# Riding projections on gate/up tails, a GpSimd memset that orders row halves, and a first norm ahead of the weight copies

## The chip, the cores and the metric

One core of one Trainium2 chip runs the kernel. The metric is the device time in microseconds of one execution, lower is better. The engines are PE (TensorE, matmuls; PEld is its weight loads), ACT (ScalarE), DVE (VectorE), POOL (GpSimd) and SP, which only issues DMAs.

## The reference

Four layers, A B A B, over x of 2048 x 576 in bfloat16, with the same weights each time they recur:

```python
x = x + _A_ref(_layernorm(x), A_wqkv, A_wo)
x = x + _B_ref(_layernorm(x), B_w_gate, B_w_up, B_w_down)
x = x + _A_ref(_layernorm(x), A_wqkv, A_wo)
x = x + _B_ref(_layernorm(x), B_w_gate, B_w_up, B_w_down)
```

A is attention with 32 heads of 18 channels. Each position looks at 8 positions, itself and every second one before it (0, 2, ..., 14 back). q, k and v come from `x @ wqkv` (576 x 1728), the output passes through `wo` (576 x 576). B is a bilinear GLU: `((x @ w_gate) * (x @ w_up)) @ w_down` with 4608 hidden channels.

## The kernel before

**Tiles and steps.** The sequence is cut into tiles of 128 rows. A step is one tile (the first four steps) or two tiles, 256 rows (all others), of one of the two A-B layer pairs; there are 18 steps, numbered j = 0 to 17. A step has an attention part (`attention(j, ...)`) and a GLU part (`glu(j, ...)`), and the attention of later steps runs beside the GLU of earlier ones. The depth of 576 is four blocks of 128 rows and a tail of 64 (KF = 4, TL = 64). So every projection onto a tile of output channels takes four full matmuls with 128 rows and one tail matmul with 64 rows. The 64-row remainder of `xnT` and of `wqkv` is held twice, in partitions 0 to 63 and 64 to 127, so a tail can use either row half of the PE array. The tail weights of gate lie in the lower half of `wgu_t`, those of up in the upper half.

**Who sets the order.** `Plan` is a list scheduler inside the kernel: every piece of work is an `op` with an engine, an estimated cost, keys it reads and writes, a priority and a margin (a time that is added to its readiness before it may be placed). `Plan.run` walks a modelled clock and issues the pieces in the order it finds. On each engine that order is then fixed, and the chip keeps it in each engine's queue. Waits between engines are semaphores that the framework adds.

**PSUM banks.** There are eight: two pairs for the GLU (`pg0/pu0`, `pg1/pu1`, called units), three accumulators for the down projection (`acc0`, `acc1`, `acct`), and one bank `pa` that the attention uses for transposes and the output projection (the first step also borrows the accumulators).

**GLU.** Hidden channels go in units. Two units form a pair: full gate matmuls and full up matmuls of the first unit (L793), then one batch of tails for both units (`tails`, L804), then full gate and up of the second unit (L793). The batch alternates gate tails in row half 0 and up tails in row half 1, in different banks. ACT copies the gate bank to `g_sb` (L815), DVE multiplies it with the up bank into `h` (L816) and thereby frees the unit. The down matmuls (L832, L834) of a pair come one pair later.

**Projections.** In `attention`, `project` takes a whole pair of units out of the same pool that the GLU uses. For a step of 256 rows there are two such calls, "q" (eight tiles of q and k: eight tails in four pairs) and "v" (four tiles of v and two tiles that hold the remaining q, k and v channels: six tails; the last tile is 64 columns wide). The matmuls are at L469. ACT, and at first DVE, empties the banks (L522, L533, L550).

**Attention's DVE work.** DVE forms the products of q and k and sums them (L580 to L590), and from the sixth step on the cross-partition sums and the spreading of the weights go through DRAM by DMA; DVE then gathers (`gather_l`, from `prod`) and multiplies v with the weights `ab` (`pv`, L714, L731). Both have a margin of 2000 ns from step 6 on.

**Start-up.** SP's queue first loads x, then the raw `wqkv`, whose columns ACT (L307), DVE (L305) and POOL (L303) copy into another order; then seven blocks of `w_down` (`wd`), the next tiles of x, `wo`, and gate and up in six chunks. PE runs warm-up matmuls (L759) meanwhile. The norm of the first tile is L358 to L376, its transposes L386.

Of the kernel before, what the change touches and what calls it, by code (L numbers as in the profile page):

```python
# [9 lines left out]
ACT = mybir.ActivationFunctionType  # L10
# [4 lines left out]

class Op:
    __slots__ = ("eng", "cost", "fn", "deps", "order", "succ", "n", "prio", "idx", "hold", "free",
                 "lat", "margin", "ready", "end", "nbytes", "use", "pair", "need", "lead", "land")


class Plan:
# [10 lines left out]
        self.warm = self.cool = None  # L32

    def op(self, eng, cost, fn, r=(), w=(), prio=1, after=None, hold=None, free=None, margin=0, nbytes=0, use=None,
           pair=None, need=None, lead=0, land=2000):
        o = Op()
        o.eng, o.cost, o.fn, o.prio, o.hold, o.free = eng, cost, fn, prio, hold, free
        o.margin, o.idx, o.succ, o.order, o.nbytes = margin, len(self.ops), [], set(), nbytes
        o.lat, o.use, o.pair, o.need, o.lead, o.land = self.LAT[eng], use, pair, need, lead, land
        d = set()  # L40
        for k in r:
            d.update(self.wr.get(k, ()))
        for k in w:
            d.update(self.wr.get(k, ()))
            d.update(self.rd.get(k, ()))
        for k in r:
            self.rd.setdefault(k, []).append(o)
        for k in w:
            self.wr[k] = [o]
            self.rd[k] = []  # L50
        d.discard(o)
        o.deps = d
        if after is not None and after not in d:
            o.order.add(after)
        for p in d | o.order:
            p.succ.append(o)
        o.n = len(d | o.order)
        self.ops.append(o)
        return o
# [10 lines left out]
    def run(self, slots):  # L70
        clock = {e: 0.0 for e in self.LAT}
        dma = 0.0
        free = {k: [(0.0, i) for i in range(v)] for k, v in slots.items()}
        cand = [o for o in self.ops if o.n == 0]
        done = 0
        while cand:
            best = None
            for o in cand:
                t = 0.0
                for p in o.deps:  # L80
                    e = p.ready if p.eng != o.eng else p.end
                    if e > t:
                        t = e
                t += o.margin
                if o.hold is not None:
                    f = free[o.hold]
                    if not f:
                        continue
                    t = max(t, min(f)[0])
                if o.pair is not None:  # L90
                    if len(free["unit"]) < len(o.pair):
                        continue
                    f = sorted(free["unit"])[:len(o.pair)]
                    t = max([t, f[0][0]] + [x[0] + 150 - o.lead for x in f[1:]])
                if o.need is not None:
                    t = max(t, o.need["at"])
                t = max(t, clock[o.eng])
                key = (t, o.prio, o.idx)
                if best is None or key < best[0]:
                    best = (key, o)  # L100
            assert best is not None, "the plan is stuck"
            (t, _, _), o = best
            cand.remove(o)
            if o.hold is not None:
                got = min(free[o.hold])
                free[o.hold].remove(got)
                o.use["slot"] = got[1]
            if o.pair is not None:
                for u in o.pair:
                    got = min(free["unit"])  # L110
                    free["unit"].remove(got)
                    u["at"], u["slot"] = got
            if o.eng == "PE" and self.warm is not None:
                if o is self.cool:
                    self.warm = None
                else:
                    self.warm(min(44, int(max(0, t - clock["PE"] - 100) / 100)))
            o.end = t + o.cost
            clock[o.eng] = o.end
            o.ready = o.end + o.lat  # L120
            if o.nbytes:
                dma = max(dma, o.end) + o.nbytes / (330.0 if dma < 60000 else 250.0)
                o.ready = dma + o.land
            if o.free is not None:
                u = o.use
                u["last"] = max(u.get("last", 0.0), o.ready)
                u["left"] = u.get("left", 1) - 1
                if u["left"] == 0:
                    free[o.free].append((u["last"], u["slot"]))
            o.fn()  # L130
            done += 1
            for s in o.succ:
                s.n -= 1
                if s.n == 0:
                    cand.append(s)
        assert done == len(self.ops)


# [1 line left out]
def kernel(  # L140
# [12 lines left out]
    nc = tc.nc  # L153
# [34 lines left out]
        return consts.tile(shape, dt, name=name)  # L188

    ident = sb("ident", [P, P])  # L190
    eps_t = sb("eps_t", [P, 1], FP32)
    cap = sb("cap", [32, W, HALO], FP32)
    wqkv = sb("wqkv", [P, KT, 3 * D])
# [69 lines left out]
    def load_x(t0, nst):  # L263
        b, i0 = (t0 // 2) % 2, t0 % 2
        if t0 == 2:
            op("POOL", 80, lambda: nc.gpsimd.memset(xb[b][0:1, i0, 0:2], 0.0), r=["wq3_0"], w=[f"xb{b}_{i0}"])
        o = op("SP", 600, dma(xb[b][:, i0:i0 + nst, :], xv[:, t0:t0 + nst, :]), w=[f"xb{b}_{i}" for i in range(i0, i0 + nst)],
               nbytes=P * nst * D * 2, prio=1.5 if t0 > 1 else 0, land=3000, after=marks.get("x") if t0 == 3 else None)
        if t0 in (2, 3):
            marks["x"] = o  # L270

# [12 lines left out]
    def setup_b():  # L284
# [6 lines left out]
        for k in range(KT):  # L291
            for t3 in (0, 1, 2, 3):
# [8 lines left out]
                rk = [f"wraw{k}"] if k < KF else ["wrawt0", f"wrawt{TL}"]  # L301
                if t3 == 3 and k < KF:
                    op("POOL", 700, lambda dst=dst, src=src: nc.gpsimd.tensor_copy(dst, src), r=rk, w=[f"wq{t3}_{k}"], prio=2)  # L303
                elif t3 % 2 == 0:
                    op("DVE", cost[0], lambda dst=dst, src=src: nc.vector.tensor_copy(dst, src), r=rk, w=[f"wq{t3}_{k}"], prio=2)  # L305
                else:
                    op("ACT", cost[1], lambda dst=dst, src=src: nc.scalar.copy(dst, src), r=rk, w=[f"wq{t3}_{k}"], prio=2)  # L307
# [131 lines left out]
    def attention(j, la, t0, nst):  # L439
# [84 lines left out]
        def grp(p_, u, m):  # L524
            return bank(p_, u)[:, 0:m * n].rearrange("p (m s) -> p m s", m=m)
        op("ACT", 250, lambda: nc.scalar.copy(vT[:, :, 0:HALO], halo_v[la][:]), r=[f"halov{la}"], w=[f"vH{z}"], prio=prio)
        mpb = 4 // nst
        if nst == 2:
            un = [[(b_, e, 512 * b_ + P * (2 * m + e), P) for b_ in range(2) for e in range(2)] for m in range(2)]
            tq = [(h_, m, un[m][2 * h_ + e]) for m in range(2) for e in range(2) for h_ in range(2)]  # L530

# [11 lines left out]
        else:  # L543
# [3 lines left out]
            tb = 1  # L547
            tq = [(h_, 0, uq[4 * h_ + e]) for e in range(4) for h_ in range(2)]
            tq += [(0, 1, uv[0]), (1, 1, ut[0]), (0, 1, uv[1]), (1, 1, ut[1]), (0, 1, uv[2]), (0, 1, uv[3])]
        ev_t = [(390, lambda u, d: nc.scalar.mul(qT[0:TL, KF, 0:n], bank(tb, u)[0:TL, 0:n], qscale), [f"q4{z}"], 0),  # L550
                (390, lambda u, d: cp(d, kT[0:TL, KF, HALO:HALO + n], bank(tb, u)[TL:P, 0:n]), [f"k4{z}"], 1),
                (390, lambda u, d: cp(d, vT[0:TL, KF, HALO:HALO + n], bank(tb, u)[0:TL, n:2 * n]), [f"v4{z}"], 0)]
        if nst == 2:
            ev_v = [(590, lambda u, d, m=m: cp(d, vT[:, 2 * m:2 * m + 2, HALO:HALO + n], grp(m, u, 2)), [f"v{2 * m}{z}"], 0) for m in range(2)]
            project("v", ut, uv, tv, ev_t, ev_v, [f"{x}{z}" for x in ("v0", "v2", "q4", "k4", "v4")])
        else:
# [82 lines left out]
        else:  # L639
# [14 lines left out]
            def soft1d():  # L654
                fold(mx_t, ALU.max)
                shift(wv(late["Lt"]))
            op("DVE", 100 + 7 * n, gather_l, r=[f"part{jj}" for jj in range(4)], w=["Lt", "prod0", "prod1"], prio=prio - 1, margin=800 if j < 6 else 2000)
            op("DVE", 240 + 4.5 * n, soft1d, w=["Lt", "mx", "prod0"], prio=prio - 1)
        op("ACT", 170 + 1.8 * n, lambda: nc.scalar.activation(late["Lt"][:, 0:W * sq], late["Lt"][:, 0:W * sq], ACT.Exp),
           r=["Lt"], w=["Lt"], prio=prio - 1)  # L660
# [43 lines left out]
        for i_ in range(W):  # L704
# [11 lines left out]
            def gather(i_=i_, half=half):  # L716
# [1 line left out]
                nc.tensor.matmul(bo[0]()[:, 0:KF * n], lhsT=ident[:], rhs=pr[:, 0:KF, 0:n], start=(i_ == 0), stop=(i_ == W - 1))  # L718
                nc.tensor.matmul(bo[1]()[:, 0:n], lhsT=ident[:], rhs=pr[:, KF, 0:n], start=(i_ == 0), stop=(i_ == W - 1))
            o = op("DVE", 60 + 3 * n, pv, r=vk + abk, w=["oT"] if to_o else [pvk], prio=prio,  # L720
                   margin=0 if on_pe or i_ else 800 if j < 6 else 2000)
            if fast:
                pl.also(o, ["prod0", "prod1"])
            if fast:
# [43 lines left out]
    def glu(j, t0, nst, last):  # L768
# [27 lines left out]
            bb("PE", 4 * ul * 0.428, fn, r=xk + fkeys(nm, fts(u)), w=[f"{nm}_{j}_{u}"], **kw)  # L796

        def tails(us):
            def fn():
                for m, first in zip(us, (False, True)):  # L800
                    s_ = units[m]["slot"]
                    for e, ft in enumerate(fts(m)):
                        for r_, ps in ((slice(0, TL), pg[s_]), (slice(TL, 2 * TL), pu[s_])):
                            nc.tensor.matmul(ps[:, e * n:(e + 1) * n], lhsT=wgu_t[r_, ft * P:(ft + 1) * P],  # L804
                                             rhs=xT[r_, KF, 0:n], start=(first and e == 0), stop=not first,
                                             skip_group_check=True)
            fl = [ft for m in us for ft in fts(m)]
            bb("PE", 190 + 225 * len(us), fn, r=xk + fkeys("wgt", fl) + fkeys("wut", fl),
               w=[f"{nm}_{j}_{m}" for nm in ("wg", "wu") for m in us], need=units[us[-1]])

        def evac(u):
            gs, hs = unit_no["n"] % 2, unit_no["n"] % NH
# [7 lines left out]
        def load_wd(g):  # L820
            b = wd_no["n"] % NWD
            wd_no["n"] += 1
            op("SP", 550, dma(wd[b][:], wd_v[g]), w=[f"wd{b}"], nbytes=P * 2 * D * 2, prio=5.5 + (g // 3 if j == 0 else 0))
            return b

        def down(u, hs, bl):
# [103 lines left out]
```

## Time and profile before

| what | value |
|---|---|
| median of three runs | 1092.41 us (1090.3 to 1092.68) |
| the profiled execution | 1094.49 us |
| its span, first to last instruction | 1092.7 us |
| mean granted PE clock in it | 0.995 |
| PE busy | 1066.9 us (98%) |
| DVE busy | 756.6 us (69%) |
| ACT busy | 368.9 us (34%) |
| POOL busy | 9.8 us (1%), none of it after 12 us |

The page names lines of the kernel. A tile's buffer number is left out, so `pg` is `pg0` or `pg1`. A row of the timeline gives start and length in us; one row can merge several equal instructions (xN). Matmuls are pipelined, so their lengths overlap: what one costs PE is the step from its start to the next start. In square brackets stands the idle time of the engine before the row, and what ended it.

### The profile page before, as it was taken

What the parts mean: (1) busy time and instruction counts of PE and PEld (TensorE: products, weight loads), DVE (VectorE), ACT (ScalarE), POOL (GpSimd) and SP (SyncE); (2) the same over time, 40 slices, a digit from 0 to 9 for tenths busy, and PEclk for the clock granted to TensorE, in tenths of its full rate; (3) what the DMA queues carried; (4) which work ended last, traced back from release to release, by engine and by line L of the source; (5) the groups of instructions that cost most, each with busy time, mean ns of one, the idle gap of its engine ahead of it and who ended that gap; (6) DMA issues with size and microseconds to landing.
All of it is one profiled execution on the core that took longest, in us unless ns stands there. A gap on an engine that the chain in (4) does not pass through costs nothing.

```text
span 1092.7 us, 25246 instructions
## 1 busy us (share of the span) xinstructions
PE 1066.9 (98%) x10636; PEld 791.5 (72%) x10793; DVE 756.6 (69%) x1344; ACT 368.9 (34%) x757; POOL 9.8 (1%) x39
## 2 busy tenths in 40 slices
PE   7999999999999999999999999999999999999998
PEld 6788877777777777777776777776777777777775
DVE  5587888595958876776949677786869587632222
ACT  5544354332331444232232424333224233122121
POOL 3000000000000000000000000000000000000000
PEclk8999999999999999999999999999999999999999
DMA  9954654635353544344462635353453536343341
GB/s 273 344 154 131 187 166 130 164 90 158 81 154 106 155 126 111 112 123 138 122 162 77 184 88 150 91 144 95 117 147 76 157 83 161 110 109 111 92 116 55
DMA packets 155089, 146.16 MB, mean 134 GB/s; under 512 B 43104, under 2 KB 152672, under 8 KB 154976
## 3 DMA queue, kind: packets, MB, share of 16 engines
q1 hardware_dynamic: 154976, 144.55, 48.0%
q8 instruction: 84, 1.38, 0.5%
q14 instruction: 29, 0.24, 0.1%
HBM read 125.11 MB, written 10.88 MB: 124 GB/s over the span
## 4 chain that ended last, share of the span: by engine, by line
PE 95%; DVE 2%; issue 1%; DMA 1%; ACT 1%; SPq 0%; DVEq 0%; ACTq 0%
PE pg L793 24%; PE pu L793 23%; PE acc L832 19%; PE pg L469 7%; PE pg L804 7%; PE acct L834 5%; PE pu L469 4%; PE pa L746 4%; DVE h L816 1%; DMA ab<-a_dram 0%; DMA wraw<-in_A_wqkv_dram 0%; ACT wqkv L307 0%; DVE prod L714 0%; DMA a_dram<-s 0%; PE pa L680 0%
## 5 line engine op out<-in xcount | busy, mean ns | idle before, releaser
L816 DVE TENSOR_TENSOR h<-pu,g_sb 128x512 bf16<-128x512 f32 x288 | 195.5, 685 | 200.6 <-ACT g_sb L815 145.1
L815 ACT CAST g_sb<-pg 128x512 bf16<-128x512 f32 x288 | 168.1, 585 | 465.4 <-PE pu L804 388.6
L793 PE MATMUL pg<-xnT_B,wg 128*128 128x256 bf16 (+1 forms) x2592 | 300.8, 261 | 0.8 <-ACT xnT_B L431 0.8
L793 PE MATMUL pu<-xnT_B,wu 128*128 128x256 bf16 (+1 forms) x2592 | 299.3, 261 | 0.0
L832 PE MATMUL acc<-wd,h 128*128 128x512 bf16 x995 | 286.4, 380 | 0.0
L793 PEld LDWEIGHTS <-wg 128*128 128x128 bf16 x2592 | 212.6, 98 | 61.2 <-issue 26.4
L793 PEld LDWEIGHTS <-wu 128*128 128x128 bf16 x2592 | 230.9, 98 | 23.3
L834 PE MATMUL acct<-wd,h 128*128 128x64 bf16 x1152 | 222.0, 193 | 8.2
L832 PEld LDWEIGHTS <-h 128*128 128x128 bf16 x1152 | 112.8, 98 | 118.1 <-issue 0.2
L714 DVE TENSOR_TENSOR prod<-vT,ab 128x1280 bf16<-128x1280 bf16 (+1 forms) x127 | 93.1, 742 | 58.6 <-DMA ab<-a_dram 58.4
L469 PEld LDWEIGHTS <-wqkv 128*128 128x128 bf16 (+1 forms) x1260 | 99.8, 100 | 37.8 <-issue 20.9
L834 PEld LDWEIGHTS <-h 128*128 128x128 bf16 x1152 | 112.9, 98 | 2.3
L580 DVE TENSOR_TENSOR prod<-qT,kT 128x2560 bf16<-128x2560 bf16 (+1 forms) x72 | 95.2, 1327 | 3.3 <-ACT kT L522 2.6
L469 PE MATMUL pg<-xnT_A,wqkv 128*128 128x256 bf16 (+4 forms) x720 | 93.8, 267 | 1.7 <-issue 1.1
L731 DVE TENSOR_TENSOR oT<-oT,prod 128x1280 bf16<-128x1280 bf16 (+1 forms) x119 | 90.9, 764 | 3.5
L804 PE MATMUL pu<-xnT_B,wgu_t 64*128 64x256 bf16 (+1 forms) x648 | 88.0, 260 | 0.0
L804 PE MATMUL pg<-xnT_B,wgu_t 64*128 64x256 bf16 (+1 forms) x648 | 88.0, 260 | 0.0
L469 PE MATMUL pu<-xnT_A,wqkv 128*128 128x256 bf16 (+5 forms) x540 | 72.9, 267 | 3.3 <-DVE h L816 3.3
L804 PEld LDWEIGHTS <-wgu_t 64*128 64x128 bf16 x1296 | 47.0, 94 | 32.2 <-issue 27.7
L746 PE MATMUL pa<-wo_p,oT 128*128 128x288 bf16 x310 | 48.2, 286 | 0.1
L375 ACT ACTIVATE xn<-xf,nmr,rstd 128x576 bf16<-128x576 f32 x47 | 40.7, 866 | 9.1 <-DVE nmr L367 8.8
L584 DVE TENSOR_TENSOR prod<-prod 128x1024 bf16<-128x1024 bf16 (+1 forms) x64 | 41.5, 648 | 0.9
(117 smaller groups left out, 561.5 us busy)
## 6 DMA issues: line engine op xcount, KB each, us to landing
wd<-in_B_w_down_dram SPq DMA_DIRECT2D x324, 288.0 KB, 3.2
s_dram<-s SPq DMA_DIRECT2D x13, 512.0 KB, 3.6
prod<-s_dram SPq DMA_DIRECT2D x52, 128.0 KB, 2.9
ab<-a_dram SPq DMA_DIRECT2D x52, 128.0 KB, 2.7
wg<-in_B_w_gate_dram SPq DMA_DIRECT2D x6, 768.0 KB, 9.4
wu<-in_B_w_up_dram SPq DMA_DIRECT2D x6, 768.0 KB, 10.3
out_dram<-ob SPq DMA_DIRECT2D x8, 288.0 KB, 2.8
wraw<-in_A_wqkv_dram SPq DMA_DIRECT2D x4, 432.0 KB, 5.1
```

Source lines behind the costliest of these rows:

```text
L469: nc.tensor.matmul(bank(p_, u)[0:m, e * n:(e + 1) * n], lhsT=wqkv[r_, k, c0:c0 + m], rhs=xnT_A[r_, k, 0:n], start=start, stop=stop, skip_g ...
L580: nc.vector.tensor_tensor(late["prod"][p_ % 2][:, :, :, 0:n], q2, k2, op=ALU.mult)
L584: nc.vector.tensor_tensor(prod[:, :, 0:4:2, 0:n], prod[:, :, 0:4:2, 0:n], prod[:, :, 1:4:2, 0:n], op=ALU.add)
L714: nc.vector.tensor_tensor(js(dst), js(vT[:, :, o0:o0 + n]), abw, op=ALU.mult)
L731: op("DVE", 60 + 3 * n, lambda i_=i_: nc.vector.tensor_tensor(oT[:, :, 0:n], oT[:, :, 0:n], late["prod"][i_ % 2][:, 0, :, 0:n], op=ALU.add ...
L746: nc.tensor.matmul(b()[:, 0:HD], lhsT=oT[:, t, i * P:(i + 1) * P], rhs=wo_p[:, t, hh * HD:(hh + 1) * HD], start=(t == 0), stop=(t == KT - 1))
L793: nc.tensor.matmul(pt[:, e * n:(e + 1) * n], lhsT=w_[:, k, ft * P:(ft + 1) * P], rhs=xT[:, k, 0:n], start=(first and k == 0 and e == 0), s ...
L804: nc.tensor.matmul(ps[:, e * n:(e + 1) * n], lhsT=wgu_t[r_, ft * P:(ft + 1) * P], rhs=xT[r_, KF, 0:n], start=(first and e == 0), stop=not ...
L815: op("ACT", 590, lambda: nc.scalar.copy(g_sb[gs][:, 0:ul], pg[use["slot"]][:, 0:ul]), r=[f"wg_{j}_{u}"], w=[f"g{gs}"], prio=0)
L816: op("DVE", 690, lambda: nc.vector.tensor_tensor(hb[hs][:, 0:ul], pu[use["slot"]][:, 0:ul], g_sb[gs][:, 0:ul], op=ALU.mult), r=[f"wu_{j}_{ ...
L832: nc.tensor.matmul(acc[i][:], lhsT=lhs, rhs=wt[:, e % 2, 0:512], start=(ft == 0), stop=(ft == NFT - 1))
L834: nc.tensor.matmul(acct[:, i * TL:(i + 1) * TL], lhsT=lhs, rhs=wt[:, e % 2, 512:D], start=(ft == 0 and i == 0), stop=(ft == NFT - 1), skip ...
```

## The change

Four things are changed.

1. From the eighth step on (`j >= 7`), the projections no longer take a pair of units. The 14 tiles of a step go in seven pairs of tiles through the bank `pa`. Such a pair is a "rider": when the planner places a gate/up tail batch of a 256-row step (`carry`) and a rider is ready, with `pa` free, it puts the rider into the same op. Then come the rider's eight full matmuls, its first tail in row half 0, the eight gate/up tails in the order half 1, half 0, and so on, and the rider's second tail in row half 1. Both tails of a rider write the same bank; a memset of a small tile `tick` on GpSimd waits for the first, and the second waits for the memset. A rider that has found no carrier 12000 ns after it is ready goes alone (`alone`), with both tails in row half 0. Seven ops on ACT per step empty the bank.
2. The margin before `gather_l` grows from 2000 to 3000 ns, that before `pv` from 2000 to 3500 ns (step 6 on).
3. The planner's figure for the landing of the first x tile falls from 3000 to 1500 ns, and the last narrow `wqkv` copy goes from ACT to DVE. In the order that results, ACT's part of the first norm stands ahead of the `wqkv` copies.
4. The loads of `w_down` may only be issued after the load of x that ends start-up (`after=marks["x"]`), so the first of them stand behind `wo` and two chunks of gate and up in SP's queue.

```diff
@@ Plan.run
+            mate = None
+            if o.carry and free["pa"] and min(free["pa"])[0] <= t + 100:
+                for r in sorted((r for r in cand if r.rider is not None), key=lambda r: r.idx):
+                    if all((p.ready if p.eng != "PE" else p.end) + r.margin / 8 <= t + 100 for p in r.deps):
+                        mate = r
+                        break
+            if mate is not None:
+                cand.remove(mate)
+                got = min(free["pa"])
+                free["pa"].remove(got)
+                mate.use["slot"] = got[1]
+                o.cost += mate.cost
...
+            if mate is not None:
+                o.fn(mate.rider)
@@ load_x
-               ... land=3000, ...
+               ... land=3000 if t0 else 1500, ...
@@ setup_b
-                elif t3 % 2 == 0:
+                elif t3 != 1:
                     op("DVE", cost[0], lambda dst=dst, src=src: nc.vector.tensor_copy(dst, src), ...
@@ attention
-        if nst == 2:
+        ride = j >= 7
+        if ride:
+            tiles = [(x, 512 * i + P * t, P, f"{x}{t // 2 * 2}") for i, x in enumerate("qkv") for t in range(KF)]
+            tiles += [("t", 1536, P, None), ("t", 1664, TL, None)]
+            for i in range(0, len(tiles), 2):
+                b = Bank()
+                def fullr(i=i, b=b):
+                    for e in range(2):
+                        _, c0, m, _ = tiles[i + e]
+                        for k in range(KF):
+                            nc.tensor.matmul(b()[0:m, e * n:(e + 1) * n], lhsT=wqkv[:, k, c0:c0 + m], ...
+                def tailr(e, half=None, i=i, b=b):
+                    _, c0, m, _ = tiles[i + e]
+                    half = e if half is None else half
+                    r_ = slice(half * TL, half * TL + TL)
+                    return nc.tensor.matmul(b()[0:m, e * n:(e + 1) * n], lhsT=wqkv[r_, KF, c0:c0 + m], ...
+                def alone(f=fullr, t=tailr):
+                    f()
+                    t(0, 0)
+                    t(1, 0)
...
+                o = op("PE", 8 * 109 + 109, alone, r=xk + ..., prio=0, margin=12000,
+                       rider=(fullr, tailr), **b.take())
...
+                op("ACT", 595 if key else 1170, evr, r=[b.key], w=dk, prio=1, **b.drop())
+        elif nst == 2:
...
-            op("DVE", 100 + 7 * n, gather_l, ... margin=800 if j < 6 else 2000)
+            op("DVE", 100 + 7 * n, gather_l, ... margin=800 if j < 6 else 3000)
...
-                   margin=0 if on_pe or i_ else 800 if j < 6 else 2000)
+                   margin=0 if on_pe or i_ else 800 if j < 6 else 3500)
@@ glu, tails
+                todo = [(m, first, e, ft) for m, first in zip(us, (False, True)) for e, ft in enumerate(fts(m))]
+                if mate is None:
+                    for a_ in todo:
+                        one(0, *a_)
+                        one(1, *a_)
+                else:
+                    mate[0]()
+                    top = mate[1](0)
+                    tk = nc.gpsimd.memset(tick[:], 0.0)
+                    for a_ in todo:
+                        one(1, *a_)
+                        one(0, *a_)
+                    sync = mybir.DependencyInfo(mybir.DependencyClass.Sync, mybir.DependencyReason.DATA)
+                    tc.add_manual_dep(tk.ins, top.ins.name, sync, reason="the bank's first row half")
+                    tc.add_manual_dep(mate[1](1).ins, tk.ins.name, sync, reason="the bank's second row half")
...
-               w=[...], need=units[us[-1]])
+               w=[...], need=units[us[-1]], carry=nst == 2)
@@ load_wd
-            op("SP", 550, dma(wd[b][:], wd_v[g]), ..., prio=5.5 + (g // 3 if j == 0 else 0))
+            op("SP", 550, dma(wd[b][:], wd_v[g]), ..., prio=5.5 + (g // 3 if j == 0 else 0), after=marks["x"])
```

## The prediction

> **What bounds the kernel now.** I read the page first, then the chain of waits, the PE waits, and the timeline where projections and gate/up tails run. All durations below are from the one profiled execution: 1094.49 us, of which 1092.7 are its span.
>
> ```profile
> PE 1066.9 (98%) x10636; PEld 791.5 (72%) x10793; DVE 756.6 (69%) x1344; ACT 368.9 (34%) x757; POOL 9.8 (1%) x39
> PE 95%; DVE 2%; issue 1%; DMA 1%; ACT 1%; SPq 0%; DVEq 0%; ACTq 0%
> PE pu L469 <- DVE h L816: 3.3, 4, 1.5
> ```
>
> PE carries the end: 95% of the chain is PE, and after 60 us its waits are few; the largest is 3.3 us, four projection tails (L469) that waited until DVE (L816) had emptied a bank. So a change is worth what it adds to or takes from PE's queue, plus start-up, plus those waits. The timeline (start, length, engine, line) shows what the matmuls with 64 rows cost:
>
> ```profile
> 470.83 1.37 PE L469 MATMUL pg<-xnT_A,wqkv 128*128 128x256 bf16 x9
> ...
> 472.67 0.61 PE L469 MATMUL pg<-xnT_A,wqkv 128*128 128x256 bf16 x4
> ...
> 484.10 1.04 PE L793 MATMUL pu<-xnT_B,wu 128*128 128x256 bf16 x8
> 485.07 0.28 PE L804 MATMUL pg<-xnT_B,wgu_t 64*128 64x256 bf16 x1
> 485.07 0.28 PE L804 MATMUL pu<-xnT_B,wgu_t 64*128 64x256 bf16 x1
> 485.19 0.27 PE L804 MATMUL pg<-xnT_B,wgu_t 64*128 64x256 bf16 x1
> ...
> 485.41 0.27 PE L804 MATMUL pg<-xnT_B,wgu_t 64*128 64x256 bf16 x1
> 485.62 1.05 PE L793 MATMUL pg<-xnT_B,wg 128*128 128x256 bf16 x8
> ```
>
> A tail for row half 0 and one for half 1 start together, and the next pair follows 0.11 us later: two for the price of one. Full matmuls step by 0.109 (eight fill the 0.87 from 483.23 to 484.10), so the last full before the batch started at 484.86; the first tail came 0.21 later, and the next full 0.21 after the last pair. Each turn between 128-row and 64-row work thus costs 0.10 beyond the step: a batch is pairs x 0.11 + 0.20.
>
> **Projections, before.** Each of the 11 steps concerned (7 to 17) has a q/k batch of four pairs, 0.44 + 0.20 = 0.64, and a v/tail batch: from 470.83 to 472.67, 1.84 us for eight fulls (0.87) and six tails, so 0.97; its turns include those of a 64-column tile. 1.61 a step, 17.7 in all.
>
> **Projections, after.** The 14 tiles go two by two through the one bank `pa`: 77 pairs of tiles. A pair rides only if a gate/up tail batch comes up, with the bank free, before its margin of 12 us is over. Pairs of gate/up units stand 6.10 us apart (485.07 to 491.18), so about two chances fall into the margin. In the built order GpSimd holds 16 `tick` memsets: 16 pairs ride, 61 go alone. Alone, both tails use row half 0 and run one behind the other. Step 0 has such a place, the `x2` row at 18.18 in the next fence: 0.28 for two of about 0.225 each, a step of 0.055, which is one full matmul of 128 columns. So two tails of 256 columns cost 0.22, plus the turns. The built order gives: 42 ordinary ones between 128-row work, 0.42 each, 17.6; 9 that run straight into a gate/up tail batch and share its turn, 0.22 each, 2.0; 10 with the 64-column tile, four turns, 0.62 each, 6.2; 15 ordinary rides at one more pair, 1.7; one ride with the 64-column tile, 0.5. Sum 28.0, **+10.3 us on PE**, nothing beside it, since PE is the path. The fulls (8 x 0.109 a pair) are the same before and after; so are the nine evacuations a step on ACT (six of 0.59, three of 0.37), which lie beside PE's work on an engine that is busy 34%, and would cost only where PE waits for the bank (below).
>
> **The wait on GpSimd.** In a ride the last tail's weight load waits for the memset, which waits for the ride's first tail. Behind it in PE's queue stand the next unit's gate and up matmuls, so all of the chain waits; behind the memset on GpSimd stands nothing. Between first and last tail lie four pair steps, 0.44. Against that: a tail's record 0.27, 0.07 until a GpSimd instruction starts on a semaphore (first memset ends 0.94, L275 starts 1.02), the memset, 0.05 until PE starts (1.31 to 1.36), and some 0.06 of weight load (estimate: the part of its 0.10 that no matmul covers). Two rows price the memset:
>
> ```profile
> 0.24 0.10 POOL L914 MEMSET const-float32-0.0<- 128x1 f32 x1 [0.24 <-issue]
> 6.63 0.56 POOL L266 MEMSET xb<- 1x2 bf16 x1
> 18.18 0.28 PE L469 MATMUL pg<-xnT_A,wqkv 64*128 64x128 bf16 x2
> ```
>
> With 0.11 the stall is 0.27 + 0.07 + 0.11 + 0.05 + 0.06 - 0.44 = 0.12; with 0.56 it is 0.57; times 16 that is 1.9 or 9.1. Below, 0 if the weight load is early. The 0.56 has the very shape, but it ran beside two DVE copies of `wqkv` (L305, 5.56 to 7.16) and ended with them at 7.19; no such copy runs after 14 us, so I take 0.11, **+1.9**.
> On this the Trainium skill's page "SBUF — State Buffer" (section "Who interferes with whom") says that a VectorE copy in a two-port mode shuts GpSimd out for the whole instruction, while a `tensor_tensor` with two SBUF inputs disturbs only a GpSimd instruction that reads SBUF. A memset only writes; by that rule it stays short beside the attention's products and the sum stays at +1.9, and by the 0.56 row it would be +9.1. The 0.56 row agrees with the first half; no run shown here has a memset beside a `tensor_tensor`.
>
> **Waits removed.** Projections no longer take the gate/up banks, so the four waits (3.3) go. The longest had a sequel:
>
> ```profile
> 754.19 0.83 DVE L714 TENSOR_TENSOR prod<-vT,ab 128x1280 bf16<-128x1280 bf16 x1 [8.62 <-DMA ab<-a_dram]
> 757.01 0.27 PE L469 MATMUL pu<-xnT_A,wqkv 64*128 64x256 bf16 x1 [1.53 <-DVE h L816]
> 757.66 1.76 PE L469 MATMUL pg<-xnT_A,wqkv 128*128 128x256 bf16 x8
> 759.22 1.91 PE L469 MATMUL pu<-xnT_A,wqkv 128*128 128x256 bf16 x8
> ```
>
> DVE stood 8.62 us before L714 for a DMA, L816 queued behind it, PE waited, and the next 17 matmuls ran at half pace (eight take 1.56 and 1.71 instead of 0.87, and 0.2 more): 1.7 us. The larger margins (3000, 3500 instead of 2000) put such DVE work later in the order, behind more L816. Together **-5.0**. What is late next: `pa`, which ACT must empty (0.6) between two lone pairs while gate and up matmuls fill PE; I put **+1.0** for these and for L816 still late now and then (0 to 3).
>
> **Start-up.** Now the first norm's Ln stands ahead of the `wqkv` copies on ACT. Before:
>
> ```profile
> 3.73 0.21 DVE L360 BATCH_NORM_AGGREGATE mv<-st 128x2 f32<-128x12 f32 x1
> 5.56 1.12 ACT L307 COPY wqkv<-wraw 128x512 bf16<-128x512 bf16 x1 [1.89 <-DMA wraw<-in_A_wqkv_dram]
> 6.59 0.29 ACT L364 ACTIVATE rstd<-mv,eps_t 128x1 f32<-128x1 f32 x1
> 8.94 0.56 PE L386 MATMUL acc<-ident,xn 128*128 128x128 bf16 x5 [2.70 <-ACT xn L375]
> ```
>
> Ln can start at 4.0 instead of 6.59, and the wait for ACT's copies between (5.56 to 6.68, 7.02 to 8.02) goes, so the transposes come at about 6.3, right behind the warm-up matmuls (end 6.24), and PE's 2.70 us of idling goes. In the windows view the granted clock was 0.50 from 10.3 to 17.15: step 0's projections ran at half pace and ended at 18.4. At full pace the limit is the last `wqkv` piece: it lands at 11.9, DVE copies it by 13.2 (L305, 12.01 + 1.15) and now the 192-column piece by about 13.5 (estimate 0.3, from 0.62 for 512), tails 0.8: 14.3. That is 4.1 earlier; up to the first gate/up matmul at 37.63 all is one chain, so it passes through. At half pace it is about 2 (PE starts about 3 earlier, copies hold it). I take **-4.0** (-2 to -5). `wd`'s first loads move behind `x`, `wo` and two gate/up chunks on SP; `x` no longer stands behind seven of them (12.96) but waits for a GpSimd memset (7.19). The bytes until the last gate/up chunk are the same, the DMA share there is near 1, and the late half of this gain may be lost to that.
>
> **Sum.** +10.3 + 1.9 - 5.0 + 1.0 - 4.0 = +4.2. On the profiled execution that is 1098.7. That run is 2.1 above the median of 1092.41 (1090.3 to 1092.68); I apply the sum to the median and take **1096.5**.
>
> **Rivals.**
> *The tails are paid back* (0.20): start-up gives its full 5, the memset hides, no new waits: 10.3 - 5.0 - 5.0 = +0.3, 1092.7. For it: every removed wait is in the trace. Against: 61 of 77 pairs alone is fixed, and one more late bank eats it.
> *Lone pairs turn for nothing* (0.18): if PE makes the turn while a lone pair's weights load, 42 x 0.20 + 10 x 0.40 = 12.4 go and the time is 1084; below 0.05 a turn it is faster than before by more than a measurement of this kernel can tell (0.2%, 2.2 us). Against: 0.10 stands in each batch of both kinds, whatever its length.
> *The memset waits for any DVE work* (0.09): DVE is busy 69%; at 0.56 a ride, +7.2, 1103.7. For it the row; against, that only copies were beside it.
> *Forecast* (0.53): slower, 1094.6 to 1099.
> That the change doesn't do what it says is partly so already: riding is the exception.
>
> **Range and chances.** Low 1090.5: the first rival with every bound at its best (memset 0, start-up and waits in full) and a fifth of the second. High 1102: the forecast with a half-pace start (+2) and half of the memset's extra price (+3.6). Left out are most of the second rival and the upper half of the third, some 0.2. Faster 0.18 (lone pairs), same 0.20 (paid back), slower 0.62.
>
> **What would show it.** Per group: lone `pa` batches 0.42 beyond their fulls; 16 gaps of about 0.1 before the last tail of a ride; L266-shaped memsets near 0.1; no L469 wait on L816 after 200 us; first gate/up matmul at 33 to 34 us, clock 1.0 from 7 us. It is wrong if lone pairs cost under 0.3, if the first gate/up matmul stays at 36 or later, or if PE waits on `pa` or on L816 for more than 4 us after 60 us.

## The result, and the profile after

| | before | after |
|---|---|---|
| median | 1092.41 us (1090.3 to 1094.35, 5 runs) | 1096.08 us (1095.84 to 1096.38, 5 runs) |
| ratio after / before, 95% interval | | 1.0037 [1.0024, 1.005], that is +4.0 us (2.6 to 5.5) |
| profiled execution, its span | 1094.49, 1092.7 | 1096.08, 1094.3 |
| first gate/up matmul starts at | 37.63 | 33.08 |
| rest: span less that start | 1055.1 | 1061.2 |

The change makes the kernel slower, by 0.4%. The last two rows split one execution of each: the start-up is 4.55 us shorter, the rest 6.1 longer.

Line numbers move: project L469 is now L491, gate/up L793 is L859, their tails L804 are L869, DVE's product L816 is L896, down L832 and L834 are L912 and L914, `pv` L714 is L780, Ln L364 is L386. New are L560 (a pair's eight full matmuls), L567 (its two tails) and L880 (`tick`).

The page of after, first its busy shares, then its chain of waits, then the group of `pv` (busy, mean ns | idle before it), with that group in before below it:

```profile
PE 1082.2 (99%) x10797; PEld 790.2 (72%) x10797; DVE 759.2 (69%) x1345; ACT 365.8 (33%) x756; POOL 10.3 (1%) x55
...
PE 97%; DVE 1%; DMA 0%; ACT 0%; issue 0%; SPq 0%; DVEq 0%; POOL 0%; ACTq 0%
...
L780 DVE TENSOR_TENSOR prod<-vT,ab 128x1280 bf16<-128x1280 bf16 (+1 forms) x127 | 92.8, 742 | 31.4 <-DMA ab<-a_dram 31.1
L714 DVE TENSOR_TENSOR prod<-vT,ab 128x1280 bf16<-128x1280 bf16 (+1 forms) x127 | 93.1, 742 | 58.6 <-DMA ab<-a_dram 58.4
```

PE still carries the end, more of it than before (97% against 95%). DVE's idling before `pv` fell from 58.6 to 31.4 us, and the kernel is slower all the same. The fall comes with riding and not with the margins: in the runs below, the idle time is 30.1 in ride_only, 63.9 in margins_only and 62.1 in no_ride. The PE waits of after from 60 us to the end have one row, where before had the four waits on L816 (3.3):

```profile
PE pa L567 <- POOL tick L880: 0.2, 1, 0.2
```

The timeline of after (start, length, engine, line) shows one lone pair, one lone pair with the 64-column tile, and one ride:

```profile
244.32 0.39 PE L567 MATMUL pa<-xnT_A,wqkv 64*128 64x256 bf16 x2
244.64 1.05 PE L859 MATMUL pu<-xnT_B,wu 128*128 128x256 bf16 x8
...
246.01 1.16 PE L560 MATMUL pa<-xnT_A,wqkv 128*128 128x256 bf16 x8
247.10 0.50 PE L567 MATMUL pa<-xnT_A,wqkv 64*128 64x256 bf16 x2
247.54 0.39 PE L912 MATMUL acc<-wd,h 128*128 128x512 bf16 x1
```

```profile
222.39 1.04 PE L560 MATMUL pa<-xnT_A,wqkv 128*128 128x256 bf16 x8
223.36 0.28 PE L567 MATMUL pa<-xnT_A,wqkv 64*128 64x256 bf16 x1
...
223.76 0.09 POOL L880 MEMSET tick<- 1x2 bf16 x1 [7.11 <-PE pa L567]
223.80 0.27 PE L869 MATMUL pg<-xnT_B,wgu_t 64*128 64x256 bf16 x1
223.91 0.28 PE L567 MATMUL pa<-xnT_A,wqkv 64*128 64x256 bf16 x1
...
224.12 0.61 PE L859 MATMUL pg<-xnT_B,wg 128*128 128x256 bf16 x4
```

The lone pair's full matmuls start at 243.35, so it takes 244.64 - 243.35 = 1.29, 0.42 beyond eight fulls (0.87). The one with the 64-column tile takes 247.54 - 246.01 = 1.53, 0.66 beyond. The ride takes 224.12 - 222.39 = 1.73; fulls and a batch without a rider are 0.87 + 0.64, so the ride adds 0.22. Half of that is the wait: the last tail belongs beside the last gate tail (223.80) and starts 0.11 after it, since the memset that it waits for began only at 223.76.

Start-up, from the same timeline (Ln, the transposes, the first projection, the first gate/up matmul):

```profile
4.15 0.29 ACT L386 ACTIVATE rstd<-mv,eps_t 128x1 f32<-128x1 f32 x1 [0.48 <-DVE mv L382]
...
5.83 0.56 PE L408 MATMUL acc<-ident,xn 128*128 128x128 bf16 x5 [0.27 <-ACT xn L397]
...
7.97 0.38 PE L491 MATMUL pg<-xnT_A,wqkv 128*128 128x128 bf16 x4 [0.86 <-ACT xnT_A L411]
...
33.08 1.05 PE L859 MATMUL pg<-xnT_B,wg 128*128 128x128 bf16 x16 [0.78 <-ACT xnT_B L453]
```

Ln starts at 4.15 instead of 6.59, PE's idling before the transposes is 0.27 instead of 2.70, and the granted clock of this run was 1.00 from 10 to 17 us, where before had 0.52.

### The profile page after: what moved, and what is told of

The parts are those of the page before. It is cut to its first block, busy times and chain, and to the rows that moved or that the text cites. A ratio compares the mean times of both kernels' runs of the same rounds, so it can differ in the third digit from the quotient of the medians.

```text
span 1094.3 us, 25407 instructions
## 1 busy us (share of the span) xinstructions
PE 1082.2 (99%) x10797; PEld 790.2 (72%) x10797; DVE 759.2 (69%) x1345; ACT 365.8 (33%) x756; POOL 10.3 (1%) x55
## 4 chain that ended last, share of the span: by engine, by line
PE 97%; DVE 1%; DMA 0%; ACT 0%; issue 0%; SPq 0%; DVEq 0%; POOL 0%; ACTq 0%
PE pg L859 24%; PE pu L859 23%; PE acc L912 23%; PE pg L869 7%; PE pa L560 6%; PE pa L812 4%; PE acct L914 3%; PE pa L567 2%; PE pg L491 2%; PE pu L491 1%; DVE wqkv L327 1%; DMA wraw<-in_A_wqkv_dram 0%; PE pu L869 0%; PE pa L746 0%; PE pa L408 0%
## 5 line engine op out<-in xcount | busy, mean ns | idle before, releaser
L896 DVE TENSOR_TENSOR h<-pu,g_sb 128x512 bf16<-128x512 f32 x288 | 196.5, 687 | 238.4 <-ACT g_sb L895 173.3
L912 PE MATMUL acc<-wd,h 128*128 128x512 bf16 x1152 | 307.7, 380 | 0.0
L859 PE MATMUL pg<-xnT_B,wg 128*128 128x256 bf16 (+1 forms) x2592 | 300.9, 261 | 0.8 <-ACT xnT_B L453 0.8
L859 PE MATMUL pu<-xnT_B,wu 128*128 128x256 bf16 (+1 forms) x2592 | 299.5, 261 | 0.0
L859 PEld LDWEIGHTS <-wg 128*128 128x128 bf16 x2592 | 212.2, 98 | 60.6 <-issue 23.9
L859 PEld LDWEIGHTS <-wu 128*128 128x128 bf16 x2592 | 229.4, 98 | 26.4 <-issue 2.7
L914 PE MATMUL acct<-wd,h 128*128 128x64 bf16 x1152 | 222.0, 193 | 0.0
L912 PEld LDWEIGHTS <-h 128*128 128x128 bf16 x1152 | 112.6, 98 | 121.9 <-issue 4.6
L780 DVE TENSOR_TENSOR prod<-vT,ab 128x1280 bf16<-128x1280 bf16 (+1 forms) x127 | 92.8, 742 | 31.4 <-DMA ab<-a_dram 31.1
L914 PEld LDWEIGHTS <-h 128*128 128x128 bf16 x1152 | 112.9, 98 | 2.0
L869 PE MATMUL pu<-xnT_B,wgu_t 64*128 64x256 bf16 (+1 forms) x648 | 88.0, 260 | 0.0
L869 PE MATMUL pg<-xnT_B,wgu_t 64*128 64x256 bf16 (+1 forms) x648 | 87.7, 259 | 0.0
L560 PE MATMUL pa<-xnT_A,wqkv 128*128 128x256 bf16 (+1 forms) x616 | 81.2, 273 | 0.0
L869 PEld LDWEIGHTS <-wgu_t 64*128 64x128 bf16 x1296 | 50.2, 94 | 27.4 <-issue 22.4
L560 PEld LDWEIGHTS <-wqkv 128*128 128x128 bf16 (+1 forms) x616 | 57.6, 99 | 12.0 <-issue 2.5
L491 PEld LDWEIGHTS <-wqkv 128*128 128x128 bf16 (+2 forms) x490 | 33.0, 98 | 11.5 <-issue 5.6
```

The costliest lines, as they stand in the source:

```text
L491: nc.tensor.matmul(bank(p_, u)[0:m, e * n:(e + 1) * n], lhsT=wqkv[r_, k, c0:c0 + m], rhs=xnT_A[r_, k, 0:n], start=start, stop=stop, skip_g ...
L560: nc.tensor.matmul(b()[0:m, e * n:(e + 1) * n], lhsT=wqkv[:, k, c0:c0 + m], rhs=xnT_A[:, k, 0:n], start=(e == 0 and k == 0), stop=False, s ...
L780: nc.vector.tensor_tensor(js(dst), js(vT[:, :, o0:o0 + n]), abw, op=ALU.mult)
L859: nc.tensor.matmul(pt[:, e * n:(e + 1) * n], lhsT=w_[:, k, ft * P:(ft + 1) * P], rhs=xT[:, k, 0:n], start=(first and k == 0 and e == 0), s ...
L896: op("DVE", 690, lambda: nc.vector.tensor_tensor(hb[hs][:, 0:ul], pu[use["slot"]][:, 0:ul], g_sb[gs][:, 0:ul], op=ALU.mult), r=[f"wu_{j}_{ ...
L912: nc.tensor.matmul(acc[i][:], lhsT=lhs, rhs=wt[:, e % 2, 0:512], start=(ft == 0), stop=(ft == NFT - 1))
```

## The experiments

The runs went to the chip in groups, each beside runs of the kernel before on the same chip; the ratio is to those. "First" is the start of the first gate/up matmul in the profiled execution, "rest" its span less that. A median holds many executions, first and rest one each.

| kernel | median, us | ratio to before [95%] | first | rest |
|---|---|---|---|---|
| before | | 1 | 37.63 | 1055.1 |
| after | 1096.08 | 1.0037 [1.0024, 1.005] | 33.08 | 1061.2 |
| start_only | 1090.32 | 0.9981 [0.9964, 0.9998] | 33.85 | 1054.2 |
| ln_only | 1091.05 | 0.9985 [0.997, 1.0] | 33.48 | 1055.3 |
| margins_only | 1090.3 | 0.9978 [0.9963, 0.9993] | 35.92 | 1052.5 |
| no_ride | 1087.86 | 0.9961 [0.9944, 0.9977] | 34.86 | 1051.7 |
| ride_only | 1100.07 | 1.007 [1.0049, 1.0091] | 36.60 | 1061.2 |
| all_lone | 1100.34 | 1.0057 [1.0039, 1.0074] | 33.76 | 1064.3 |
| one_half | 1097.09 | 1.0031 [1.0019, 1.0043] | 34.41 | 1061.1 |
| more_rides | 1091.38 | 0.9997 [0.9987, 1.0007] | 33.37 | 1055.8 |
| full_row | 1087.26 | 0.9939 [0.9923, 0.9956] | 33.02 | 1052.4 |
| v_full | 1090.61 | 0.9972 [0.996, 0.9984] | 33.28 | 1054.1 |
| full_row_wide | 1082.82 | 0.9926 [0.9905, 0.9947] | 37.34 | 1049.5 |
| v_full_wide | 1084.54 | 0.9937 [0.9917, 0.9956] | 35.30 | 1047.8 |

**The theory.** Riding costs more PE time than the batches that it replaces, nearly all of it in the lone pairs, and the margins and the new start-up pay only part of it. The rivals: lone pairs turn between 128 and 64 rows for nothing; the wait on GpSimd is the loss; the parts pay each other back. The change was first taken apart.

### The start-up edits alone (start_only)

```diff
 before, load_x
-  land=3000
+  land=3000 if t0 else 1500
 before, setup_b
-  elif t3 % 2 == 0:
+  elif t3 != 1:
 before, load_wd
-  op("SP", ..., prio=...)
+  op("SP", ..., prio=..., after=marks["x"])
```

> The kernel before with the start-up part of the change alone (landing figure 1500 for the first x tile, last narrow weight copy on DVE, w_down loads behind the x load); projections and margins as before. Theory: start-up is worth what the two traces show, the first gate/up matmul at 32.1 instead of 37.6, so 5.5 us, all passed on to the end: 1092.4 - 5.5 = 1087 (1086 to 1088.5). Rival (the gain is eaten by weights that land late in the first GLU step): first gate/up at 32, but waits on DMA between 35 and 60 us and 1090 or more.

Measured: 0.9981, 2.1 us faster (0.2 to 3.9); in the profiled executions 3.8 earlier at the first gate/up matmul. The direction holds; by the medians the size is about half of the prediction's 4.0, and less than half of the 5.5 expected here. The time came out at the rival's 1090, but the rival's reason is not there: in the profiled execution PE waits for no DMA between 30 and 62 us, and some 600 gate/up matmuls later it is still 3.9 us ahead of before (114.9 against 118.8). Start-up differs from execution to execution, and the last section shows by how much. My text put the first gate/up matmul of after at 32.1; that is its first weight load, and the matmul starts at 33.08, so the gain in the traces is 4.55 and not 5.5.

### The first norm without the moved loads (ln_only)

```diff
 start_only, load_wd
-  op("SP", ..., prio=..., after=marks["x"])
+  op("SP", ..., prio=...)
```

> The kernel before with the first norm ahead of the weight copies alone (planner's figure 1500 for the first x tile, the last narrow wqkv copy on DVE), the loads of w_down where they were. Theory: the start-up gain is the norm's, and the loads' new place only moves transfers that end at the same time: as start_only, ratio 0.998, first gate/up matmul at 33 to 35 us. Rival, that the seven loads of w_down ahead of x, wo and the first gate/up chunks hold the later part of start-up: first gate/up matmul at 36 us or later, ratio 1.000.

Measured: 0.9985 against 0.9981 of start_only, first gate/up matmul at 33.48 against 33.85. The start-up gain is the norm's; where the seven `wd` loads stand makes no difference that shows.

### The margins alone (margins_only)

```diff
 before, attention
-  gather_l, ... margin=800 if j < 6 else 2000
+  gather_l, ... margin=800 if j < 6 else 3000
-  pv, ... 800 if j < 6 else 2000
+  pv, ... 800 if j < 6 else 3500
```

> The kernel before with the two larger margins alone (3000 and 3500). Theory as predicted: they put the DVE work that waits for a DMA behind the emptying of gate/up banks, so the waits of L469 on L816 (3.3 us) and the clock drop behind the longest (1.7) go: 1088 to 1090. Rival: the waits come from projections that take both gate/up units, whatever DVE does first; the margins change little: 1091.5 to 1093, L469 still waiting on L816.

Measured: 0.9978, 2.4 us faster (0.8 to 4.0). The waits of PE from 60 us on:

```profile
PE pu L469 <- DVE h L816: 2.2, 4, 0.8
```

They shrink from 3.3 to 2.2 and the long one (1.5) goes. So the time is about the theory's, but only a third of the waits goes; that L469 still waits on L816 is what the rival said.

### Start-up and margins without riding (no_ride)

```diff
 after, attention
-  ride = j >= 7
+  ride = False
```

> The changed kernel with projections in the gate/up units as before (no riders, no memsets); start-up and margins changed. Theory: the riding part alone costs the +10.3 us of PE work and about 2.1 us of waits on the memset (16 gaps of 0.11 to 0.46 in the trace), and saves at most 3.3 of waits on L816: 1096.1 - 12.4 + (0 to 3.3) = 1083.7 to 1087. Rival (lone pairs turn for nothing, the loss sits elsewhere): no more than 3 us below the changed kernel, 1093 or more.

Measured: 0.9961 [0.9944, 0.9977], 4.3 us faster, about the sum of start_only and margins_only (2.1 + 2.4). The median of 1087.9 is 0.9 above the stated range, and the rival falls. So everything in the change but riding makes the kernel faster, and riding takes 0.76% of the time, 8.3 us, on top of no_ride.

### Riding alone (ride_only)

```diff
 before: all of Plan.run, attention and tails from the change (20 rides, 57 lone pairs);
 margins, load_x, setup_b and load_wd as before
```

> The kernel before with the riding part alone (start-up and margins as before); its built order has 20 rides and 57 lone pairs. Theory: +9.5 us of PE tail work (the built order by the same prices), +2.4 of memset waits, -3.3 to -5 of bank waits: 1092.4 + 7 to 9 = 1099 to 1101. Rival (lone pairs turn for nothing): 1088 to 1091.

Measured: 1.007, 7.6 us slower, and the rival with 1088 to 1091 falls. Its PE waits from 60 us on are one row of 0.2 on `tick`, with the old margins: leaving the units' banks is enough to end the waits on L816. Its rest is 1061.2, that of after. It has four more rides, worth some 0.8 us by the prices below, so beside riding the margins bring at most about that.

### What a ride is worth: all_lone, more_rides, one_half

```diff
 all_lone: after, glu
-  carry=nst == 2
+  carry=False
 more_rides: after, attention and Plan.run (52 ride, 25 go alone)
-  margin=12000
+  margin=32000
-  ... + r.margin / 8 <= t + 100
+  ... + 1500 <= t + 100
 one_half: after, tails
-  top = mate[1](0)
-  tk = nc.gpsimd.memset(tick[:], 0.0)
+  mate[1](0, 0)
...
-  tc.add_manual_dep(tk.ins, ...); tc.add_manual_dep(mate[1](1).ins, tk.ins, ...)
+  mate[1](1, 0)
```

> The changed kernel (1096.1 us) with carry=False: no ride and no memset, all 77 pairs of tiles go alone. Theory: a ride costs 0.11 us for its pair of tails and 0.11 for the wait on GpSimd, a lone pair 0.42; 16 x 0.2 = 3 us slower, 1099. Rival, that a ride costs nothing beyond its pair of tails: 16 x 0.31 = 5 slower, 1101. Rival, that the wait takes all that riding saves: 1096.

> The changed kernel with a margin of 32000 instead of 12000 ns before a rider goes alone (a carrier may still take it from 1500 ns on): 52 pairs ride, 25 go alone, instead of 16 and 61. Theory: a ride costs 0.22 with its wait on GpSimd, a lone pair 0.42, one that runs into a tail batch 0.22: 36 more rides give back 4 to 7 us, 1089 to 1092, with 52 waits of 0.11 on L880's memset, and not below no_ride (1087.9), whose batches cost 0.23 a pair. Rival, that a ride costs only its pair of tails: 36 x 0.31 = 11, 1085. Rival, that projections that come 20 us later make DVE's attention work late: no gain, 1096 or more.

> The changed kernel with the same 16 rides, but both tails of the rider in row half 0, the first and the last of the batch: no memset, no second tail beside another one. Theory: the last tail runs alone behind a tail of its own row half, 16 x 0.11 = 1.8 us more PE work, and the 16 waits of 0.11 go: no difference, 1096, and a steady gap of 0.11 before the last tail in each ride. Rival, that the wait on GpSimd costs 0.5 or more a ride: 1090 or less.

Measured: without rides the rest grows by 3.1 us (by the ratios 2.2, with intervals that overlap): 16 x 0.20, as the theory has it. By the ratios alone the rival's 5 would only just fall; the rows above, 0.42 for a lone pair and 0.22 for a ride, decide it. With 52 rides the rest falls by 5.4 and the ratio is 0.9997 [0.9987, 1.0007]. That lies inside 4 to 7 and short of the 11 that a ride without a wait would give. Its 52 memsets, from the view by source line:

```profile
L880 POOL MEMSET tick<- x52: 89/90/91, 216.6 to 924.3; 1x2 bf16 x52
```

Even so it only comes back to before: a ride at 0.22 is no cheaper than a pair in the old batches (1.61 / 7 = 0.23), and the price of the 25 lone pairs takes up about what start-up gained. one_half, with no memset and no wait, has a rest of 1061.1 and a ratio of 1.0031 against 1.0037, no difference. Its timeline has the gap before the last tail that the wait makes in after, here as PE work behind a tail of the same row half:

```profile
431.55 0.27 PE L869 MATMUL pg<-xnT_B,wgu_t 64*128 64x256 bf16 x1
431.66 0.27 PE L567 MATMUL pa<-xnT_A,wqkv 64*128 64x256 bf16 x1
431.86 1.05 PE L859 MATMUL pg<-xnT_B,wg 128*128 128x256 bf16 x8
```

So the GpSimd link is not the loss: it costs what the one tail would cost that it lets run beside another.

### Whether a lone pair's turns cost: full_row

```diff
 all_lone, attention
+  if j == 7:
+      op("ACT", 1500, lambda: nc.scalar.mul(wqkv[:, KF, 0:3 * D], wqkv[:, KF, 0:3 * D], 0.5), ...)
 tailr
-  r_ = slice(half * TL, half * TL + TL)
+  r_ = slice(0, P)
```

> As all_lone, and before step 7 ACT halves the tail weights of wqkv once, so that each projection tail of steps 7 to 17 is a 128-row matmul over both copies of the 64-row remainder (half plus half is the whole sum). No lone pair turns to 64 rows any more. Theory, that a turn costs 0.10: a lone pair's tails cost 2 x 0.109 = 0.22 instead of 0.42 (0.62 with the 64-column tile), 77 x 0.22 = 16.8 instead of 28.0 in the changed kernel, and its 2 us of ride waits go: 13 less, 1083. Rival, that lone pairs turn for nothing: only the ride waits go, 1094.

```profile
300.27 1.04 PE L563 MATMUL pa<-xnT_A,wqkv 128*128 128x256 bf16 x8
301.14 0.38 PE L569 MATMUL pa<-xnT_A,wqkv 128*128 128x256 bf16 x2
301.36 0.38 PE L914 MATMUL acc<-wd,h 128*128 128x512 bf16 x1
...
313.19 1.16 PE L563 MATMUL pa<-xnT_A,wqkv 128*128 128x256 bf16 x8
314.28 0.51 PE L569 MATMUL pa<-xnT_A,wqkv 128*128 128x256 bf16 x2
314.72 1.05 PE L861 MATMUL pu<-xnT_B,wu 128*128 128x256 bf16 x8
```

Line numbers in this run and the next two are two or three higher than in after (L563 and L569 are a pair's fulls and tails, L914 is down, L861 gate/up). The number of matmuls is the same, with 128 rows in the tails: a lone pair takes 301.36 - 300.27 = 1.09 instead of 1.29. Against all_lone the rest falls by 11.9 us, 0.18 for each of 66 ordinary pairs, those included that run straight into a tail batch and save nothing. The rival (1094) falls: a lone pair's turns cost 0.20. My 1083 was missed by 4: I had priced the pair with the 64-column tile at 0.22 like the others, and its last three rows show 314.72 - 313.19 = 1.53, no less than in after.

### The same tails in the old batches (v_full), and the 64-column tile widened (full_row_wide, v_full_wide)

```diff
 v_full: no_ride, project (and the tail weights of columns 1024 to 1727 halved once in step 4)
-  mm(..., slice(half * TL, half * TL + TL), ...)
+  mm(..., slice(0, P) if tag == "v" and j >= 4 else slice(half * TL, half * TL + TL), ...)
 full_row_wide: full_row, attention; v_full_wide: v_full, likewise for steps 4 to 17
-  ("t", 1664, TL, None)
+  ("t", 1600, P, None)
-  nc.scalar.copy(vT[0:TL, ...], b()[0:TL, n:2 * n])
+  nc.scalar.copy(vT[0:TL, ...], b()[TL:P, n:2 * n])
```

> The changed kernel without riding (no_ride, 1087.9), and ACT halves the tail weights of v and of the last two tiles once in step 4, so that the six tails of the v batch in steps 4 to 17 are 128-row matmuls. Theory: six x 0.109 = 0.65 instead of 0.97 in each of 14 steps, 4.4 us less: 1083.5, faster than both kernels. Rival, that the turns of a batch hide behind something else: 1088.

v_full missed: 1090.6, and its rest is 2.4 longer than that of no_ride. A v batch of v_full, from its first full matmul (L491) to what follows its last tail:

```profile
473.16 1.37 PE L491 MATMUL pg<-xnT_A,wqkv 128*128 128x256 bf16 x9
474.37 0.27 PE L491 MATMUL pu<-xnT_A,wqkv 128*128 128x256 bf16 x1
474.48 0.71 PE L491 MATMUL pg<-xnT_A,wqkv 128*128 128x256 bf16 x3
475.03 0.27 PE L491 MATMUL pu<-xnT_A,wqkv 128*128 128x256 bf16 x1
475.14 0.78 PE L815 MATMUL pa<-wo_p,oT 128*128 128x288 bf16 x5
```

475.14 - 473.16 = 1.98 for 14 matmuls that step by 0.109, 1.53 in all. The row turns are gone and 0.45 remains: the 64-column tile's fulls and its tail stand between 128-column ones, four turns of columns at 0.11. A rival would be that a 64-column matmul is slower as such. Matmul by matmul, the trace speaks against it: the four 64-column fulls start at 473.69, 473.82, 473.93 and 474.04, so within the run they step by 0.11 to 0.13, and the steps of about 0.20 to 0.23 stand only where the width changes. In no_ride the same batch took 1.84.

> As v_full (1090.6), and the 64-column tile of steps 4 to 17 widened to 128 columns. In v_full the eight full matmuls and six tails of a v batch took 1.98 us, 0.45 more than 14 x 0.109 and 0.14 more than the 1.84 of no_ride, since the tail of the 64-column tile stood alone between wide ones. Theory: all four column turns go, 14 x 0.45 = 6.3 less, 1084.3, some 3.5 below no_ride (1087.9). Rival, that v_full lost its time to waits on DVE: 1089 or more.

> As full_row (1087.3), and the last tile of a step is widened from 64 to 128 columns (1600 to 1727; it computes k's remainder a second time, and the copy to vT reads the upper half). Theory, that a turn between 128 and 64 columns costs 0.10 like one between row counts: the pair with that tile took 1.53 from start to the next start in full_row where the others take 1.09; 11 x 0.44 = 4.8 us less, 1082.4, the fastest of all. Rival, that the column turns hide: 1087.

Both came out as the theory had them. v_full_wide has a rest 6.3 us below v_full (14 x 0.45), the median is 1084.5. PE's waits on DVE beyond 60 us are no shorter in it than in v_full (2.6 and 2.3 us), so the rival falls. full_row_wide has a rest 2.9 below full_row and a median of 1082.8, 4.4 below it, where 4.8 was expected; with 0.9926 it has the lowest time of the study, 8 us below before, though the interval overlaps with that of v_full_wide. Its one profiled execution (1088.6) was one with a lower clock in start-up, in the windows view (the number after the engines is the granted clock):

```profile
17.00:24.00 7.00, 5.15 (x122) 4.52 (x120) 5.78 (x12) 3.98 (x13) 0.00 (x0) 0.76 0.99 314
45.00:52.00 7.00, 5.64 (x68) 4.84 (x69) 2.73 (x7) 2.84 (x9) 0.00 (x0) 0.76 1.08 332
```

The second row lies in the rest, and full_row has 1.00 there: 7 x 0.24 = 1.7 us, most of what the 2.9 lack to 4.8.

## Why the prediction was right, point by point

The forecast of 1096.5 and the time of 1096.08 agree, and the case that was the likeliest is the one that happened. The mechanism, lone pairs that pay for their turns, is shown. That the sum came within 0.4 us is in part luck: in the profiled pair, from whose first half the terms were worked out, it is +1.6 and not +4.2. Term by term:

**Projection tails, +10.3: right.** The rows of after give 0.42 for a lone pair (0.42 forecast), 0.66 with the 64-column tile (0.62), 0.11 for a ride's pair. full_row takes the turns between row counts away and has 11.9 us less in the rest than all_lone; its edit changes the tails and adds one ACT instruction. Here the Trainium skill's page "TensorEngine Tiling (Array Packing)", section "Key Properties", says that a change of tiling mode drains TensorE. The rows agree in that each change costs time, and add the price, 0.10 to 0.11 a turn, for columns as for rows.

**The wait on GpSimd, +1.9: right.** All 16 memsets took 89 or 90 ns (forecast 110, rival 560). In weight-load starts, 13 of the 16 rides have 0.55 from the first tail to the last where four pair steps are 0.44; the others have 0.49, 0.65 and 0.89. Together that is 2.1 us. Not all of it is the memset's time: the 0.65 is the ride with the 64-column tile, with a turn more, and in the 0.89 the memset started 0.35 later than in the others, released by a gate tail. Four of the 16 memsets lay wholly inside a DVE `tensor_tensor` with two SBUF inputs, and so did 29 of the 52 of more_rides; none took longer than 91 ns. The rule of the Trainium skill's page "SBUF — State Buffer" that the prediction weighed agrees with that. one_half shows that taking the wait away in this way wins nothing.

**Waits removed, -5.0, and new waits, +1.0: together too small in the profiled pair.** No new wait came. In the weight-load rows of before, PE loses about 4.6 us beyond 60 us at six places (576, 636, 696, 757, 761 and 818 us), against the steps of the same shapes elsewhere, and 1.7 in the stretch of lower clock after 757: 6.3, of which the prediction had counted 5.0. After has none left but the rides'. The rest fits: 10.3 + 2.1 - 6.3 = 6.1, the measured difference (the 0.66 of the ten lone pairs with the 64-column tile would add 0.4). What did it was put half wrong. Leaving the banks ends these waits by itself (ride_only); the margins take only a third of them (margins_only), so the two don't add up.

The 1.7 was read as a sequel of the long wait. That is not shown. start_only has nearly the same wait, and the next matmuls ran at the full clock; here are its row and the 5 us behind it in the windows view, and under them the 5 us behind the long wait of before:

```profile
754.09 0.27 PE L469 MATMUL pu<-xnT_A,wqkv 64*128 64x256 bf16 x1 [1.35 <-DVE h L816]
...
754.00:759.00 5.00, 4.91 (x45) 3.75 (x46) 4.86 (x8) 2.74 (x8) 0.00 (x0) 1.00 0.14 36
...
757.00:762.00 5.00, 4.99 (x29) 3.25 (x29) 4.86 (x7) 2.90 (x8) 0.00 (x0) 0.66 0.00 0
```

The granted clock was 1.00 there and 0.66 in before. The 1.7 were thus seen once, and how often they come was not tried.

**Start-up, -4.0: right in the profiled pair, too large at the medians.** The traces give -4.55. But the profiled execution of before had the longest start-up of the three with the old order (37.63, 36.60, 35.92), and start_only is worth 2.1 at the medians (0.2 to 3.9). The sum in the profiled pair is thus 6.1 - 4.55 = +1.6 (spans 1092.7 to 1094.3), not +4.2. At the medians it is +4.0, so waits and start-up together took 10.3 + 2.1 - 4.0 = 8.4 there. With the start_only of the medians that is 6.3 + 2.1; without the 1.7 of lower clock it is 4.6 + 3.8, and 3.8 is what the trace of start_only shows, against the longest start-up of before. Which split is right stays open. By the first, the step "I apply the sum to the median" hid two errors of opposite sign: start-up was worth 1.9 less than forecast, and the waits 2.3 more net. By the second, start-up was nearly right and the errors are smaller.

**The rivals.** "Lone pairs turn for nothing" falls with the rows of after (1.29 a pair) and with full_row. "The memset waits for any DVE work" falls with the 16 memsets. "The tails are paid back" was close in the profiled pair (+1.6), but the interval of the ratio, [1.0024, 1.005], excludes it.

## What to carry to other kernels

A change of tile shape on PE has a price of its own, so a few small matmuls that are cheap inside a batch are dear alone: 0.42 us against 0.23 a pair here. Before tails are spread out or paired by a semaphore, try padding them to the full shape. With the 64-row remainder taken as 128 rows (weights halved, both copies used) and the 64-column tile computed 128 wide, PE did more arithmetic, and the kernel took 1082.8 us where the two others took 1092.4 and 1096.1. The padding is not all of it: the same kernel has the start-up edits and the margins, which alone bring no_ride to 1087.9.

## What the runs showed of the hardware that was not expected

The column turns: two tiles of which the second is 64 columns wide take 0.44 more than two 128-column tiles (1.53 against 1.09 in full_row), although the wide one computes half of its columns a second time.

The clock in start-up differs between executions with the same start-up edits. In all three profiled executions with the old start-up the clock from 10 to 17 us was below 1 (0.52, 0.69, 0.82), and the first gate/up matmul came at 37.63, 36.60 and 35.92, in the order of the clock. Of eleven with the new one, eight had 1.00 from 10 to 31 us and came at 33.0 to 34.4; three had a dip, to 0.75 in the lowest seven microseconds, and came at 34.9 to 37.3. One profiled execution of each kernel is therefore not enough to price a start-up edit here. What decides whether a dip comes was not tried.
